# Attention followed by a cosine layer: a fixed order for the layer's second pass, product sums in PSUM, and a plain first sum for weight pair 0

## The chip, the cores and the metric

The kernel runs on one NeuronCore of a Trainium2 chip. The metric is the device time of one execution in microseconds (us), lower is better. The engines are named as in the profile: PE (TensorE, matrix products; PEld is its weight loading), DVE (VectorE), ACT (ScalarE), POOL (GpSimd) and SP (SyncE, which issues most DMAs). PE, DVE and ACT reach PSUM, the banks that matmuls write; POOL works on SBUF alone.

## The reference

Causal attention over 4 batches, 12 heads, 448 positions and 64 columns a head, then a layer with a cosine, all in fp32:

```python
scores = q @ k.T / 8; scores[above the diagonal] = -1e9
x = softmax(scores) @ v            # laid out as 1792 tokens x 768
h = x @ w_in                       # 768 x 2048
g = h * cos(h)
out = g @ w_out                    # 2048 x 768
```

The two weights arrive as 8-byte floats; the kernel reads them as pairs of 32-bit words.

## The kernel before, in words

**Numbers in two parts.** Each fp32 operand of the layer is held as a high part (a cast, made by ACT) and a low part (the rest, by POOL or DVE), both of the type fp32r. A product is three matmuls: high x high, high x low, low x high. `split` (line 594) makes the parts of an activation.

**Attention** (lines 214 to 561) runs 24 pairs of heads, one iteration of its loop each, and three iterations (i = 24, 25, 26) that empty its pipeline. It writes x in two tiles, `xa` for tokens 0 to 1023 and `xb` for 1024 to 1791. After each iteration the loop at lines 1078 to 1101 converts one half of a piece of the first four weight blocks (two of w_in, two of w_out: "weight pair 0"), stores the raw w_out pieces (line 1086) and loads the next piece. In iterations 24 and 25 PE also does the first sums of tokens 0 to 511 (`fill`). Lines 549 to 560 compute four sums q4 of the blocks of w_in's pair 0 on DVE, split them and store them.

**Pass one** (`moe`, `slot`, lines 817 to 878) covers tokens 0 to 1023 in two groups of 512. There are eight weight pairs (two blocks of 128 of the 2048 columns), so sixteen slots k. A slot does the first sum of its group for both blocks (`m1_sum`, 18 matmuls of 512 columns each), the cosine (`cosine_stages`, lines 573 to 585: ACT index, DVE remainder, ACT Sin and Square, DVE final step) and, behind them, the second sum of the slot before (`m2a_chunk`, four chunks of 12 matmuls of 384 columns, with one `add` on DVE each; chunks alternate between two pairs of PSUM banks). Beside that it prepares the weights of the next pair: loads (`fetch`), three mask stages on ACT (line 156, 158, 160), a pack on DVE (lines 167, 171, 175), the two parts (`halve`), the sums of blocks (`first_side`, `side_out`) and the sums of x blocks for pass two (`x_side`). All of it is stored to DRAM. `first_spill` (line 770) stores the four blocks of pair 0 in slots 1 and 2, through SP.

**Pass two** covers tokens 1024 to 1791 as two halves of 384. Each first sum and each second sum is a 2 x 2 product of blocks, done with seven block products instead of eight (Strassen's scheme in Winograd's form), at the price of sums of blocks on both sides. The orders are `SIDE` (first sum) and `MO` (second sum). A round g does these parts:

- `m1b(g)`: seven products of nine matmuls (line 952). The first is copied by ACT to p1 (line 966); `plus` adds the others, on DVE, into SBUF tiles u2, u3, p1, c12, c21, c22; two of the four cosines begin there, reading these tiles.
- `factors`: the other cosines, four sums s1 to s4 of the results on POOL, seven splits (ACT, POOL) into `g_ops`.
- `block_sums(g)`: four sums of the raw w_out blocks on POOL (line 937), from a tile `raw` that is loaded for each pair, with casts on ACT and low halves on DVE or POOL (line 939).
- `m2b(g)`: 21 products of three matmuls (line 1010) in pairs of PSUM banks, each pair added into `accs` by DVE (line 652 through `add`).

Pair 7 is last and is done plainly (`m2_last`), after `combine` has added the 21 accumulators up (line 1025, POOL and DVE).

**What sets the order.** Attention and pass one are inside `with tc.manual_schedule()` (line 1073), so each engine runs them in the order in which the program names them. Pass two runs outside of it (line 1105). There the framework orders the instructions by its own planning, and products of the next round stand between blocks of this one where that planning put them. SP's DMAs have one queue in program order.

Of the kernel before, what the change touches and what calls it, by code (L numbers as in the profile page):

```python
# [20 lines left out]
def kernel(  # L21
# [51 lines left out]
    t_d = spill.tile([9, P, 2, EH], F32, name="t_d")  # L73
# [106 lines left out]
    def spill_halves(kind, f, w, eng=nc.gpsimd):  # L180
        if kind:
            eng.dma_start(out=w_out_d[f], in_=f32(w[:]))
        elif f % 2 == 0:
            eng.dma_start(
                out=w_in_d[f // 2, :, 0:4].rearrange("p b n -> p (b n)"),
                in_=f32(w.rearrange("p u n -> p (u n)")),
            )
        else:
            eng.dma_start(out=side(f // 2, 3), in_=f32(w[:, :, EH:]))

# [23 lines left out]
    def attention(filler):  # L214
        with (
# [261 lines left out]
            for i in range(N + 3):  # L477
# [71 lines left out]
                if i == N:  # L549
                    q4 = at.tile([P, 4, EH], F32, tag="pb", bufs=2, name="q4")  # L550
                    for n, (f, b) in enumerate(((1, 0), (1, 1), (0, 0), (0, 1))):
                        w = ring[0, f][:, :, b * EH : (b + 1) * EH]
                        nc.vector.tensor_tensor(q4[:, n], f32(w[:, 0]), f32(w[:, 1]), op=ALU.add)
                    nc.vector.tensor_tensor(q4[:, 1], q4[:, 0], q4[:, 1], op=ALU.add)
                    nc.vector.tensor_tensor(q4[:, 0], q4[:, 2], q4[:, 0], op=ALU.subtract)
                if i == N + 1:
                    nc.vector.tensor_tensor(q4[:, 2], q4[:, 1], q4[:, 2], op=ALU.subtract)
                    nc.vector.tensor_tensor(q4[:, 3], q4[:, 3], q4[:, 2], op=ALU.subtract)
                    for n, b in ((1, 4), (0, 6), (2, 5), (3, 2)):
                        store_parts(split(q4[:, n], *part_tiles()), side(0, b))  # L560
# [12 lines left out]
    def cosine_stages(hv, n, d=None):  # L573
        ni = gpool.tile([P, 512], I32, tag="ni", bufs=2, name="ni")[:, 0:n]
        r = gpool.tile([P, 512], F32, tag="r", bufs=3, name="r")[:, 0:n]
# [7 lines left out]
        d = r if d is None else d  # L583
        nc.vector.scalar_tensor_tensor(d, r, 1.0, hv, op0=ALU.subtract, op1=ALU.mult)
        yield d
# [51 lines left out]
    def moe(ring, early):  # L637
        with tc.tile_pool(name="mo", bufs=1) as mo:
# [99 lines left out]
            def x_side(i):  # L738
                for t, dst, parts in x_sums:
                    hi, lo = parts or part_tiles()  # L740
                    nc.scalar.copy(hi, t)
                    nc.vector.tensor_tensor(lo, t, f32(hi[:] if parts is None else hi), op=ALU.subtract)
                    if parts is None:
# [392 lines left out]
```

## Time and profile before

| | us |
|---|---|
| three runs of the kernel before | 675.88, 679.0, 681.26 (median 679.0) |
| the profiled execution | 682.1 |
| its span, first to last instruction | 680.3 |
| attention, to the first matmul of pass one | 0 to 172.4 |
| pass one, to the end of its last first sum | 172.4 to 448.7 |
| rest of pass one and pass two | 448.7 to 680.3 |

Rows below have times from the span's start. In a group of instructions, "x54 | 49.4, 946" means 54 instructions, 49.4 us of busy time and a mean of 946 ns; after the second bar stands the idle time of that engine just before them and what ended it. In a timeline, a time in brackets is the idle time before, with its releaser. "out<-in" names the tiles. PE's matmul rows overlap, so their spacing is read from starts. The granted clock (PEclk) is a share of 2.4 GHz.

### The profile page before, as it was taken

The numbers are of one execution on the slowest core, as the hardware profiler recorded it, in microseconds if no ns is written. First come the engines' busy times: TensorE is split into PE (matmuls) and PEld (weight loads), VectorE is DVE, ScalarE is ACT, GpSimd is POOL, SyncE is SP. The second block draws the span as 40 slices with busy tenths as digits, with TensorE's granted clock in tenths as the row PEclk, the third lists the DMA queues.
The fourth block names the chain that finished last, engine by engine and source line by source line (L and its number), as shares of the span: only waits on it lengthen the run. The fifth ranks groups of instructions, "written<-read, shape, count | busy, mean of one in ns | idle before, by whom it ended". The sixth has DMA issues, their size and how long they took to land.

```text
span 680.3 us, 11579 instructions
## 1 busy us (share of the span) xinstructions
PE 640.6 (94%) x3700; PEld 555.2 (82%) x3700; DVE 507.8 (75%) x1102; ACT 429.8 (63%) x958; POOL 441.3 (65%) x425
## 2 busy tenths in 40 slices
PE   8999999999987979999999999999689979999994
PEld 6676776766766969998989899999689879989993
DVE  5888888888537756777777777733886896888796
ACT  5999898989646577777777777530643444545240
POOL 3665666656236767687968796810698987765554
PEclk9999999999987989999999999999979989999997
DMA  5555555455136965878777778599947475564303
GB/s 129 118 116 123 138 123 127 116 127 136 59 96 252 330 242 176 292 241 297 251 265 253 289 252 286 224 370 401 354 116 227 144 254 146 182 208 117 117 1 139
DMA packets 123788, 133.29 MB, mean 196 GB/s; under 512 B 73008, under 2 KB 107936, under 8 KB 123728
## 3 DMA queue, kind: packets, MB, share of 16 engines
q1 hardware_dynamic: 116912, 107.31, 50.8%
q0 software_dynamic: 4928, 24.78, 10.1%
q10 hardware_dynamic: 1888, 0.46, 0.3%
q8 instruction: 30, 0.49, 0.3%
q14 instruction: 30, 0.25, 0.1%
HBM read 82.58 MB, written 49.94 MB: 195 GB/s over the span
## 4 chain that ended last, share of the span: by engine, by line
PE 56%; DVE 14%; POOL 10%; issue 9%; DMA 6%; ACT 4%; POOLq 0%; DVEq 0%; ACTq 0%
PE banks L664 13%; PE banks L436 6%; PE banks L952 5%; PE banks L341 5%; PE banks L569 4%; PE banks L571 4%; PE banks L570 4%; PE banks L1010 4%; PE banks L412 3%; DMA w_in_d<-sh 3%; POOL tr L937 3%; PE banks L350 3%; PE banks L314 3%; DMA raw<-raw_d 3%; DVE acc L652 2%
## 5 line engine op out<-in xcount | busy, mean ns | idle before, releaser
L652 DVE TENSOR_TENSOR acc<-acc,banks 128x768 f32<-128x768 f32 x122 | 111.4, 929 | 46.0 <-PE banks L664 39.9
L664 PE MATMUL banks<-w,gh 128*128 128x384 f32 x512 | 116.4, 350 | 12.5 <-DVE acc L650 4.7
L664 PEld LDWEIGHTS banks<-w,gh 128*128 128x128 f32 x512 | 95.6, 198 | 16.0 <-DVE acc L652 5.8
L390 POOL TENSOR_TENSOR pb<-pb,stat 128x768 f32<-128x768 f32 (+2 forms) x72 | 73.9, 1040 | 42.9 <-ACT flat L324 20.1
L596 POOL TENSOR_TENSOR gl<-r,gh 128x512 fp32r<-128x512 f32 (+1 forms) x48 | 58.9, 1230 | 48.4 <-ACT gh L595 31.1
L372 ACT ACTIVATE pb<-pb,stat 128x384 f32<-128x384 f32 (+1 forms) x144 | 72.4, 511 | 16.1 <-DVE stat L358 16.1
L569 PE MATMUL banks<-xa,w 128*128 128x512 f32 x192 | 75.0, 391 | 0.0
L571 PE MATMUL banks<-xa,w 128*128 128x512 f32 x192 | 75.0, 391 | 0.0
L570 PE MATMUL banks<-xa,w 128*128 128x512 f32 x192 | 75.0, 390 | 0.0
L664 PE MATMUL banks<-w,gl 128*128 128x384 f32 x256 | 67.7, 346 | 0.0
L358 DVE CUSTOM_DVE_ANT_0 pb<-banks,mask 128x384 f32<-128x384 f32 (+1 forms) x144 | 52.9, 418 | 16.6 <-PE banks L341 16.6
L686 POOL TENSOR_TENSOR w<-ct,w 128x768 fp32r<-128x768 f32 x28 | 51.8, 1850 | 10.8 <-DVE r L578 10.2
L1010 PE MATMUL banks<-big,gh 128*128 128x384 f32 x168 | 45.2, 354 | 6.0 <-DVE cs L959 2.7
L1010 PE MATMUL banks<-big 128*128 128x384 f32 x189 | 42.9, 359 | 7.6 <-ACT big L938 5.8
L952 PE MATMUL banks<-xb,bb 128*128 128x384 f32 x261 | 49.6, 335 | 0.3 <-DVE acc L652 0.3
L580 ACT ACTIVATE r<-r 128x512 f32<-128x512 f32 (+1 forms) x64 | 36.9, 576 | 20.4 <-DVE r L578 20.2
L664 PEld LDWEIGHTS banks<-w,gl 128*128 128x128 f32 x256 | 48.6, 197 | 0.2 <-POOL gl L596 0.2
L436 PE MATMUL banks<-pm,vn 128*64 128x448 f32 (+3 forms) x384 | 46.8, 386 | 0.3
L952 PEld LDWEIGHTS banks<-xb,bb 128*128 128x128 f32 x261 | 45.6, 188 | 0.7 <-DVE acc L652 0.6
L436 PEld LDWEIGHTS banks<-pm,vn 128*64 128x64 f32 x384 | 25.4, 136 | 23.1 <-issue 13.0
L1010 PEld LDWEIGHTS banks<-big 128*128 128x128 f32 x189 | 35.9, 204 | 9.9 <-ACT big L938 6.4
L571 PEld LDWEIGHTS banks<-xa,w 128*128 128x128 f32 x192 | 36.0, 188 | 7.6
(154 smaller groups left out, 1565.0 us busy)
## 6 DMA issues: line engine op xcount, KB each, us to landing
bb<-w_in_d SPq DMA_DIRECT2D x50, 384.0 KB, 4.8
land<-in_moe_w_in_dram SPq DMA_DIRECT2D x14, 768.0 KB, 5.2
land<-in_moe_w_out_dram SPq DMA_DIRECT2D x14, 768.0 KB, 5.9
w_out_d<-w POOLq DMA_DIRECT2D x14, 768.0 KB, 5.8
big<-w_out_d SPq DMA_DIRECT2D x25, 384.0 KB, 4.0
w_in_d<-sh SPq DMA_DIRECT2D x32, 192.0 KB, 4.3
w_in_d<-sl SPq DMA_DIRECT2D x32, 192.0 KB, 3.6
w_in_d<-w POOLq DMA_DIRECT2D x7, 768.0 KB, 4.6
```

The source lines that it names most:

```text
L358: nc.vector.tensor_tensor_reduce(out=dst, in0=src, in1=m, scale=-1.0, scalar=3.0e38, op0=ALU.add, op1=ALU.min, accum_out=st[:, 0, n : n + 1],)
L372: nc.scalar.activation(dst, dst, AF.Exp, scale=-1.0, bias=st[:, 0, n : n + 1], accum_out=st[:, 1, n : n + 1],)
L390: nc.gpsimd.tensor_tensor(dst, dst, r.to_broadcast(list(dst.shape)), op=ALU.mult)
L436: nc.tensor.matmul(o[heads(j), kc * P : S], lhsT=vn[:, kc, heads(j)], rhs=pm[:, kc, j, kc * P : S], start=(kc == 0), stop=(kc == NB),)
L569: yield nc.tensor.matmul(hv, lhsT=wh[:, f], rhs=x[:, 0, cc, t], start=(cc == 0), stop=False)
L570: yield nc.tensor.matmul(hv, lhsT=wh[:, f], rhs=x[:, 1, cc, t], start=False, stop=False)
L571: yield nc.tensor.matmul(hv, lhsT=wl[:, f], rhs=x[:, 0, cc, t], start=False, stop=(cc == NCC - 1))
L596: nc.gpsimd.tensor_tensor(lo, r, f32(hi), op=ALU.subtract)
L652: nc.vector.tensor_tensor(d, d, o, op=ALU.subtract)
L664: nc.tensor.matmul(o[:, e, 0:EH], lhsT=a[:, cs], rhs=w[:, e * EH : (e + 1) * EH], start=(x == 0), stop=(x == 5),)
L952: nc.tensor.matmul(o, lhsT=w[:, u, k * P : (k + 1) * P], rhs=x[k][:, v], start=k + n == 0, stop=k == K - 1 and n == 2,)
L1010: nc.tensor.matmul(o[:, b % 2, 0:EH], lhsT=g_ops[i][u][:, c * P : (c + 1) * P], rhs=wouts[g, i][:, v], start=(x == 0), stop=(x == 2),)
```

## The change

In the attention, the q4 sums and their stores go. Each weight block of pair 0 is stored through SP as soon as its last piece is converted there (`spill_halves` in the loop after the iteration), and `first_spill` goes. The third mask stage of the first weight moves from slot 1 to iteration 26. `x_side` stores four kinds of sums in place of three (`t_d` has 12 entries; block b12 of x is kept and loaded over later).

Pass two moves inside the manual order. Its first sum for pair 0 is plain (`plain`, four sums of 18 matmuls on the weight blocks themselves), placed between the last four chunks of pass one. `late_in` issues the loads of pair 0's second sum and of pair 1 after the first sum of slot 15. Each round then has seven steps; a step is one product of the next pair (`product(nx, n)`, nine matmuls), then three products of the second sum (`blocks(g, n)`, nine matmuls), with cosines, sums and loads written out between them. The last sum of each of the four results is added in PSUM (`plus(o, o, ...)`) and the cosine reads it there. The first block of `MO` is now 3. `combine` becomes `merge` calls, five of 21 of them in the last round; the last pair's products are `m2_part`, its outputs `m2_out`.

```diff
-    t_d = spill.tile([9, P, 2, EH], F32, name="t_d")
+    t_d = spill.tile([12, P, 2, EH], F32, name="t_d")
...
-                if i == N:
-                    q4 = at.tile([P, 4, EH], F32, tag="pb", bufs=2, name="q4")
...
-                    for n, b in ((1, 4), (0, 6), (2, 5), (3, 2)):
-                        store_parts(split(q4[:, n], *part_tiles()), side(0, b))
...
-    def cosine_stages(hv, n, d=None):
+    def cosine_stages(hv, n, r=None):
...
-            SIDE = [0, 5, 6, 4, 1, 2, 3]
-            MO = [0, 3, 4, 5, 6, 1, 2]
+            SIDE = [0, 5, 6, 4, 1, 2, 3]
+            MO = [3, 0, 4, 5, 6, 1, 2]
...
+                win_ring.append(tx.pop())
+                for i in (0, 1, 4, 3):
+                    load_in(0, i)
+                for i in range(2 * K):
+                    load_x(tx[i], i)
+                load_in(1, SIDE[0])
+
+            def late_in():
...
+                first_raw()
+                load_out(0)
+                for i in range(3):
+                    load_block(0, i)
+                for i in range(1, 6):
+                    load_in(1, SIDE[i])
+                for i in range(2 * K, 3 * K):
+                    load_x(tx[i], i)
...
-                    some(opening[0])
                     mb = opening[1]
                 run(pack(ia, mo))
-                first_spill()
...
                 run(m1_sum(ring, g, 1, t0, n, hv[1]))
+                if k == 2 * NG - 1:
+                    late_in()
...
+            def plain(f, j, b):
+                o = banks8[:, b, 0:TH]
+                for k in range(2):
+                    w = wins[0, ((0, 1), (4, 3))[f][k]]
+                    for h, x in enumerate(old_x(k, j)):
+                        for n, (u, v) in enumerate(((0, 0), (0, 1), (1, 0))):
+                            nc.tensor.matmul(
...
+            o = plain(0, 1, 2)
+            chunk(0)
+            begin("21", o)
+            go("21")
+            chunk(1)
+            go("21")
+            o = plain(1, 1, 3)
+            for i in range(K):
+                load_x(b12[i], 3 * K + i)
+            chunk(2)
+            begin("22", o)
+            go("22")
+            chunk(3)
+            go("22")
...
-            load_raw(0)
-            load_out(0)
-            load_rest(0)
-            block_sums(0)
-            ready = m1b(0)
-            for g in range(NG):
...
+            for g in range(NG - 1):
+                last = g == NG - 2
+                nx = g + 1
+                load_out(nx)
...
+                sub(nx, 4)
+                a21 = end("21")
+                go("12")
+                w_hi(nx, 4)
+                go("12")
+                fetch_in(0)
+                nc.scalar.copy(p1, product(nx, 0))
+                s1 = less(sm0, a21, c_of["22"], ALU.add)
+                s2 = less(sm1, s1, c_of["11"])
+                hi(g_ops[4], s1)
+                hi(g_ops[5], s2)
+                blocks(g, 0)
+                a12 = end("12")
+                lo(g_ops[4], s1)
+                s3 = less(sm2, c_of["11"], a21)
+                lo(g_ops[5], s2)
...
+                w_lo(nx, 4, nc.vector)
...
+                plus(u2, product(nx, 1), p1)
+                blocks(g, 1)
+                sub(nx, 5)
...
+                plus(u3, product(nx, 2), u2)
+                blocks(g, 2)
+                s4 = less(sm0, a12, s2)
+                sub(nx, 3)
...
+                w_hi(nx, 3)
...
+                o = product(nx, 3)
+                plus(u2, o, u2)
+                plus(o, o, u3)
+                begin("22", o)
+                blocks(g, 3)
+                w_lo(nx, 3, nc.vector)
+                go("22")
+                go("22")
+                sub(nx, 6)
+                w_lo(nx, 5)
+                w_hi(nx, 6)
+                if last:
+                    merge(5, 0, nc.gpsimd)
+                fetch_in(4)
+                if g + 2 < NG - 1:
+                    load_raw(g + 2)
+                o = product(nx, 4)
+                plus(o, o, p1)
+                begin("11", o)
+                blocks(g, 4)
+                r = end("22")
+                go("11")
+                go("11")
+                hi(g_ops[3], r)
+                w_lo(nx, 6)
+                lo(g_ops[3], r)
...
+                o = product(nx, 6)
+                plus(o, o, u3)
+                begin("12", o, c21)
+                blocks(g, 6)
...
+                if half == 1 and j == PARTS - 1:
+                    spill_halves(*key, ring[key], nc.sync)
...
+            elif i == B * NP + 2:
+                some(opening[0])
         run(filler)
-        mixture = moe(ring, early)
-        next(mixture)
-    run(mixture)
+        moe(ring, early)
```

Of the helpers, `begin(name, o)` issues a cosine's index on ACT, the first `go` its remainder on DVE, the second `go` Sin and Square on ACT, and `end` its final step on DVE. `hi` is a cast on ACT and `lo` a low half, on POOL unless an engine is named; `less` is a sum on POOL; `sub`, `w_hi` and `w_lo` make one sum of raw w_out blocks, its cast and its low half. In step 5 (left out) the same is done for "21" as in step 4 for "11", and "11" is ended, cast and given its low half.

## Rows read from the trace of the kernel before

**Rows 1.** The page, busy time of each engine over the span.
```profile
PE 640.6 (94%) x3700; PEld 555.2 (82%) x3700; DVE 507.8 (75%) x1102; ACT 429.8 (63%) x958; POOL 441.3 (65%) x425
```

**Rows 2.** Windows: each engine's busy time (count), then PEclk, DMA share, GB/s.
```profile
200.00:210.00 10.00, 5.34 (x18) 4.80 (x17) 8.29 (x10) 5.96 (x10) 4.86 (x5) 0.67 0.58 181
440.00:460.00 20.00, 20.00 (x105) 18.56 (x105) 7.43 (x9) 5.34 (x9) 5.00 (x5) 1.00 0.99 370
448.73:676.51 227.78, 207.59 (x1114) 199.04 (x1112) 173.53 (x241) 90.10 (x190) 149.74 (x137) 0.95 0.59 197
```

**Rows 3.** Chain that ended last, whole span: start, us, what.
```profile
227.20 13.04 DMA w_in_d<-sh
...
448.89 4.18 PE banks L664 x24
```

**Rows 4.** Timeline of PE, second sums in the opening of pass one.
```profile
194.84 0.87 PE L664 MATMUL banks<-w,gh 128*128 128x384 f32 x4
...
199.28 1.65 PE L664 MATMUL banks<-w,gh 128*128 128x384 f32 x4 [3.21 <-ACT gh L595]
...
209.91 1.65 PE L664 MATMUL banks<-w,gh 128*128 128x384 f32 x4 [4.66 <-DVE acc L650]
...
216.55 0.39 PE L569 MATMUL banks<-xa,w 128*128 128x512 f32 x1
...
241.30 0.87 PE L664 MATMUL banks<-w,gh 128*128 128x384 f32 x4
...
249.88 1.65 PE L664 MATMUL banks<-w,gh 128*128 128x384 f32 x4 [4.24 <-DVE acc L652]
...
256.98 0.39 PE L569 MATMUL banks<-xa,w 128*128 128x512 f32 x1
```

**Rows 5.** Timeline of DVE in the same stretch.
```profile
178.46 1.96 DVE L553 TENSOR_TENSOR q<-w 128x384 f32<-128x384 f32 x4
...
208.90 0.95 DVE L650 TENSOR_SCALAR acc<-banks 128x768 f32<-128x768 f32 x1
```

**Rows 6.** Timeline of ACT in the same stretch.
```profile
182.31 0.41 ACT L147 CAST w<-ct 128x256 fp32r<-128x256 f32 x1 [3.05 <-DVE ct L146]
...
199.13 0.81 ACT L160 ACTIVATE banks<-flat 128x768 f32<-128x768 f32 x1
```

**Rows 7.** DMA issues: count, KB each, median us from issue to landing.
```profile
raw<-raw_d SPq DMA_DIRECT2D x7, 768.0 KB, 6.1
...
w_out_d<-w SPq DMA_DIRECT2D x2, 768.0 KB, 9.0
```

**Rows 8.** Groups by form, 482 to 650 us (rounds of pass two).
```profile
L652 DVE TENSOR_TENSOR acc<-acc,banks 128x768 f32<-128x768 f32 x54 | 49.4, 946 | 5.3 <-PE banks L1010 5.2
...
L937 POOL TENSOR_TENSOR tr<-raw 128x384 f32<-128x384 f32 x14 | 15.8, 1128 | 6.3 <-DMA raw<-raw_d 5.1 <-DVE big L939 1.2
...
L581 ACT ACTIVATE r<-r 128x384 f32<-128x384 f32 x28 | 14.5, 518 | 0.3
...
L578 DVE SCALAR_TENSOR_TENSOR r<-ni,cs 128x384 f32<-128x384 int32 x13 | 12.2, 940 | 1.2 <-ACT ni L576 0.6 <-POOL cs L986 0.4
...
L959 DVE TENSOR_TENSOR u<-banks,u 128x384 f32<-128x384 f32 x14 | 7.7, 552 | 2.2 <-PE banks L952 1.9
```

**Rows 9.** Timeline of all engines: POOL and DVE side by side, then each alone.
```profile
551.64 2.65 POOL L937 TENSOR_TENSOR tr<-raw,tr 128x384 f32<-128x384 f32 x2
...
553.35 1.36 DVE L578 SCALAR_TENSOR_TENSOR r<-ni,cs 128x384 f32<-128x384 int32 x1
...
623.92 0.55 DVE L578 SCALAR_TENSOR_TENSOR r<-ni,acc 128x384 f32<-128x384 int32 x1
...
628.01 1.99 POOL L596 TENSOR_TENSOR gl<-r,gh 128x384 fp32r<-128x384 f32 x2 [6.71 <-ACT gh L595]
```

**Rows 10.** Groups by form, 650 to 682 us.
```profile
L1025 DVE TENSOR_TENSOR acc<-acc 128x384 f32<-128x384 f32 x9 | 10.4, 1188 | 0.2 <-POOL acc L1025 0.2
```

**Rows 11.** Timeline of DVE, its last instruction.
```profile
676.54 0.55 DVE L1042 TENSOR_TENSOR acc<-acc,banks 128x384 f32<-128x384 f32 x1 [2.38 <-PE banks L1036]
```

More of the change, by code (lines that the diff above doesn't have):

```diff
@@ L637, in moe @@
     def moe(ring, early):
+        pend = None
         with tc.tile_pool(name="mo", bufs=1) as mo:
@@ new lines, in chunk, with begin, go, end @@
+            def chunk(c):
+                m2a_chunk(*pend, c)
+            c_of = {}
+            def begin(name, o, r=None):
+                c_of[name] = cosine_stages(o, TH, r)
+                some(c_of[name])
+            def go(name):
+                some(c_of[name])
+            def end(name):
+                (c_of[name],) = c_of[name]
+                return c_of[name]
+            o = plain(0, 1, 2)
[3 more added lines that the diff above has]
+            chunk(1)
@@ L1000, in pair_bank, with blocks @@
-            def pair_bank():
-                b = bank("q", 4, 6, 0, 2)
-                return banks8[:, b : b + 2]
-            def m2b(g):
-                for b in range(21):
-                    i, c = MO[b // 3], b % 3
+            def pair_bank(*places):
+                b = bank("q", *(places or (6, 4)))
+                return banks8[:, b : b + 2]
+            pair = []
+            def blocks(g, n):
+                i = MO[n]
+                for c in range(K):
+                    b = 3 * n + c
@@ new lines, in m2_part @@
+            def m2_part(j, c, o, f, gs):
+                es = [slice(e * EH, (e + 1) * EH) for e in range(2)]
+                gh, gl = gs
+                for x, (a, u) in enumerate(((gh, 0), (gh, 1), (gl, 0))):
+                    for e in range(2):
+                        nc.tensor.matmul(
+                            o[:, e, 0:EH], lhsT=a[:, c * P : (c + 1) * P],
+                            rhs=wouts[NG - 1, f, u][:, es[e]],
+                            start=f == j and x == 0, stop=f == 1 - j and x == 2,
+                        )
@@ new lines, in m2_out @@
+            def m2_out(j, c, o, rows):
+                i = (TA + j * TH) // P + c
+                for e in range(2):
+                    d = part(rows[e], c)
+                    nc.vector.tensor_tensor(d, d, o[:, e, 0:EH], op=ALU.subtract)
+                    nc.sync.dma_start(
+                        out=out[i * P : (i + 1) * P, e * EH : (e + 1) * EH], in_=d
+                    )
+            o = plain(0, 0, 4)
+            begin("11", o)
+            sub(0, 4)
+            r = end("22")
@@ new lines, in moe @@
+            hi(g_ops[3], r)
+            lo(g_ops[3], r)
+            go("11")
+            w_hi(0, 4)
+            go("11")
+            w_lo(0, 4, nc.vector)
+            sub(0, 5)
+            w_hi(0, 5)
+            o = plain(1, 0, 0)
+            load_in(1, SIDE[6])
+            load_raw(1)
+            sub(0, 3)
+            r = end("11")
+            hi(g_ops[0], r)
+            lo(g_ops[0], r)
+            w_hi(0, 3)
+            w_lo(0, 5)
+            sub(0, 6)
+            w_hi(0, 6)
@@ new lines, in moe @@
+            r = end("21")
+            ps = []
+            for c, b in enumerate((6, 4, 2)):
+                o = banks8[:, b : b + 2]
+                m2_part(1, c, o, 1, g_ops[3])
+                ps.append(o)
+            go("12")
+            hi(g_ops[6], r)
+            lo(g_ops[6], r)
+            go("12")
+            r = end("12")
+            merge(6, 5, nc.gpsimd, (2,))
+            hi(g_ops[1], r)
+            lo(g_ops[1], r)
+            merge(3, 6, nc.gpsimd)
+            merge(1, 0, nc.gpsimd)
```

314 lines of the change are left out of this document (151 added, 163 removed).

## The prediction

> **What bounds the kernel now.** I read the page's engine totals first, then the windows, then TensorE's timeline, then the groups. PE is busy for 94% of the span [rows 1], so a change can only win what PE stands idle, what it runs at the low clock, and what the end adds. Pass two holds most of it. From 448.73 us, where the last first sum of pass one ends, to PE's last matmul the stretch is 227.8 us long [rows 2]. It holds 96 matmuls of pass one's second sums and 1,017 of pass two (504 in first sums, 441 in block products, 72 for the last pair). Matmuls of 384 columns stand 0.174 us apart, since 24 of them take 4.18 us [rows 3], so 1,113 need 193.7 us: 34 us are lost there. The opening of pass one loses time as well: the first 48 matmuls of its second sum take 21.7 us (194.84 to 216.55) and the third 48 take 15.7 (241.30 to 256.98) [rows 4], where 48 x 0.174 is 8.4. That is 13.4 + 7.3 = 20.7 us. Some of it is stall (3.2, 4.7 and 4.2 us in [rows 4]), the rest is matmuls at a lower granted clock behind the stalls (0.67 on the mean from 200 to 210 us, between its levels of 1.2 and 2.4 GHz, [rows 2]).
>
> **Edit 1, the side sums of weight pair 0 leave the attention's end.** Eight VectorE operations q4 go (the first four take 1.96 us, [rows 5]), and four splits with eight stores. They hold the conversion that ScalarE waits 3.05 us for, and behind it, in queue order, the first cosine [rows 6]. The third mask stage of the first weight moves too, from behind the second cosine's cast (199.13, [rows 6]) to the attention's last iteration. Followed through by the same durations, ScalarE reaches that stage at about 187.8, VectorE starts to pack at 191.7, and its sums, two more packs and two cosines later, bring the first add to 200.7 instead of 208.90 [rows 5]. PE reaches the third chunk at 194.84 + 24 x 0.174 = 199.0 and waits for that add until 201.6: 2.6 us of the 13.4 stay, and I allow 0.8 for the clock, so 10 us are won. Bounds: 8 if the late chain shifts by its first cause only, 13.4 if nothing waits.
>
> **Edit 2, the first spills move into the attention.** Four transfers leave the first slots, two of them 768 KB from w, landing in 9.0 us [rows 7]. They crowd the queue where ScalarE's cast into a store tile waits 13.04 us for that tile's store [rows 3], which ends in the 4.24 us stall. Without them most of the second loss goes: 7 of 7.3, bounds 0 and 7.3. In the attention they stand on SP ahead of the next loads of q, k and v and of the next weight piece, and SP waits there for GpSimd's low half. Those loads run an iteration ahead of their use, which hides them as long as the queue is emptier there than in the slots. If that cover is gone, each spill costs at most about a third of the 9.0 us that it lands in: bounds 0 and 12 for the four, I take 1. Edits 1 and 2 together: 16 us earlier, between 0 and 20.
>
> **Edit 3, the passage to pass two.** The plain first sum of pair 0 needs eight half products where seven stood: 72 matmuls for 63, 9 x 0.174 = +1.6 us. It needs no sums of inputs, so 4 x 18 matmuls can be placed between the last four chunks of pass one. Loads are early: the four plain weight blocks go first, and about 24 transfers of 384 KB plus eight stores of outputs follow, some 13 MB, which 370 GB/s [rows 2] carries in 35 us, the time until the second product of pair 1. PE could start the first round at 448.73 + (96 + 72) x 0.174 = 477.9. But GpSimd gets its first sums, low halves and casts one behind the other. Counted through at 1.0 us each, w_lo(0, 6) ends near 483.5, and the third block product of round 0 starts 3 us late. The raw weights of pair 1, whose tile is free only when the last chunk has been read, are due at that same moment, 6.1 us after their issue [rows 7]. So +3 (bounds 0 and 8): rounds start at 480.9 on the old clock.
>
> **Edit 4, the seven rounds.** One round is 126 matmuls, 21.9 us on PE. The other engines, by [rows 8]: VectorE ten adds of 0.946, one of half size, eight cosine steps, seven sums and two low halves of 0.55, 19.4; GpSimd seventeen operations at 1.0, 17; ScalarE twenty-four at 0.52, 12.5. So PE is the longest, if nothing loops back. Cosines now read the sum in PSUM. With two SBUF operands a VectorE step beside a busy GpSimd takes 1.36 us and GpSimd's own 1.33; alone, a step takes 0.55 and two GpSimd operations 1.99, so 1.02 each and 0.97 from start to start [rows 9]; with a PSUM operand 0.552 on the average of all [rows 8]. Ten such pairs a round shrink to two (the low halves of blocks 3 and 4), so I take 1.0 for GpSimd (bounds 0.97 and 1.33). For the new in-place sum in PSUM there is no row: 0.55 by the nearest, 1.36 as the other end, on an engine with 2 us to spare. The Trainium skill (Perfetto Trace Analysis, section Optimizing Scalar/DVE Operations) gives VectorE about 60 ns of overhead on SBUF and 125 on PSUM; by that rule eight cosine steps would add 0.5 us a round, 3.6 us in all if it were on the path, and the sum would be 647. The rows show no such difference.
>
> The loop that could be longer than 21.9 runs from GpSimd's third block sum of one round to that of the next: thirteen ScalarE operations (casts, indices, Sin, Square) and the VectorE steps between them, 8.3 us at 0.42 to 0.58 each, then a low half, t4, s1, s2 and eight more on GpSimd, 12 x 0.97 = 11.6, and 0.5 us of waiting for the cast of s1: 20.4 us. That is 1.5 under PE's 21.9, so PE sets the pace, but with banks freed only 0.5 to 1.4 us before their next product. I take 22.5 a round (bounds 21.9 and 25.5): 7 x 22.5 = 157.5, so the last round's matmuls end at 638.4. Loads are 12 transfers of 384 KB a round, under 220 GB/s. The raw tile's reload has 7.2 us from its release (2.1 us into this loop) to its next use (9.3) against 6.1 median [rows 7]: just covered; a late one costs its lateness, about 1 us.
>
> **Edit 5, the end.** Of 21 block additions five move into the last round. From PE's last block product: VectorE's rest of adds and two cosine steps to 3.4, six additions at 1.19 [rows 10] to 10.6, six final subtractions at 0.5 [rows 11] to 13.6, three additions to 15.6, six more subtractions to 18.6. GpSimd's seven additions (ending at 11.6) and PE's 72 matmuls (12.5) lie beside it. From the end of the last subtraction to the span's end it is 3.2 us now (677.1 to 680.3, [rows 11]). So 21.8 us (bounds 20 and 25).
>
> **The sum.** 638.4 + 21.8 = 660.2, less 16 from edits 1 and 2 gives a span of 644.2. The profiled execution ran 682.1 with 680.3 of span, 1.8 around it, so 646.0. It lies 3.1 above the median of the three runs, 679.0, so I forecast 643 us.
>
> **Rivals.**
> A, the forecast: PE sets the rounds and the opening's stalls go. Its own range goes from 630 (20 won before pass two, no late start, 21.9 a round, an end of 20) to 655 (12 won, 2 us more at the start, 23.3 a round).
> B, the fixed order is set by GpSimd's loop. At 1.30 apart twelve or thirteen operations add 4.3 us to 20.4, and with a raw tile 0.8 late it is 25.5 a round: 643 + 7 x 3.0 = 664. For it: GpSimd waits 5.1 us for raw tiles now and its mean is 1.13 there [rows 8]. Against: what slows it are VectorE steps with two SBUF operands, and they go.
> C, the opening gains nothing: the spills delay the attention by as much as they free, or the store tiles wait on (three more x sums are stored). Then 16 us stay: 659, and with 12 us on the attention 671. For it: the DMA queue is on the chain at 227.20 [rows 3]. Against: the stall follows two transfers that leave.
> D, slower than before: the change does not do what it says, since in a fixed order the two rings of waits become one. VectorE's adds wait for PE's block, the cosine behind an add in VectorE's queue waits with it, its cast and low half follow late, and PE waits for the bank that the cosine frees. If each round catches two crossings of 3.1 us (a product and a block) on top of B's 24.7, a round is 30.9 and the time 643 + 7 x 8.4 = 702. It is slower from 22.5 + 36 / 7 = 27.6 us a round. For it: the trace shows one late conversion holding four later ScalarE operations [rows 6]. Against: the queue positions counted above leave each bank free in time.
> The Trainium skill (PSUM — Partial Sum Buffer, section Engine vs sequencer instructions) says that ScalarE's, VectorE's and GpSimd's queues are strictly first in, first out; D is that rule at its worst, and the trace agrees with the rule by those 3.05 us.
>
> **How the numbers follow.** A 0.72, B 0.12, C 0.12, D 0.04. The range 630 to 668 takes in A and B, C's 659, and leaves out D, the worst of C and the worst of B. About 1% can be told from no change: faster than 672 holds A, B and nearly all of C, 0.93; within 1% the worst of C and a round near 27, 0.03; slower D, 0.04.
>
> **What would show it.** Edit 1: the first add of pass one near 200 and under 3 us of PE idle there. Edit 2: no PE stall in the third slot, an attention that ends within 1 us of before. Edit 3: PE without gaps until the first round, then about 3 us. Edit 4: starts of product 0 (the copy to p1) 22 to 23 us apart, VectorE's cosine steps at 0.55, GpSimd near 1.0, a granted clock of 1.0 (2.4 GHz) through the rounds. Edit 5: about 22 us behind the last block product. It is wrong if rounds are over 25.5 us apart, if the attention ends over 3 us late, or if GpSimd's mean stays above 1.15.

## The result and the profile after

The changed kernel takes 645.0 us (median of four runs, 644.46 to 646.04), the kernel before beside it 678.6. The ratio is 0.951, 95% interval 0.947 to 0.955. Forecast were 643.0 us. The profiled execution took 644.5 us with a span of 642.7. Its totals answer to [rows 1], and under them stand the waits of TensorE over the whole span (line and what it waited for: us in total, times, longest).

```profile
PE 623.8 (97%) x3709; PEld 545.0 (85%) x3709; DVE 485.8 (76%) x1087; ACT 427.0 (66%) x953; POOL 428.8 (67%) x421
```

```profile
PE banks L1016 <- DVE r L574: 3.1, 1, 3.1
PE banks L655 <- DVE acc L641: 2.6, 1, 2.6
PE banks L1054 <- DVE acc L1064: 2.0, 1, 2.0
PE banks L316 <- DMA land<-in_q_dram: 1.2, 2, 0.7
...
PE banks L1054 <- ACT ni L567: 1.0, 1, 1.0
...
PE banks L655 <- DVE acc L643: 0.7, 1, 0.7
```

L655 is the second sum of pass one, L1016 a product of a round, L1054 the last pair. PE waits 3.1 us once, in the passage to pass two, and never inside the rounds (L1036, the block products, isn't in the list).

The opening, TensorE's timeline, answers to [rows 4]. The first line is the first chunk, the second the third chunk, the third the same place of the third 48 matmuls.

```profile
196.38 0.87 PE L655 MATMUL banks<-w,gh 128*128 128x384 f32 x4
...
203.35 0.97 PE L655 MATMUL banks<-w,gh 128*128 128x384 f32 x4 [2.62 <-DVE acc L641]
...
237.52 0.98 PE L655 MATMUL banks<-w,gh 128*128 128x384 f32 x4 [0.69 <-DVE acc L643]
```

Before, these stalls were 3.2 and 4.7 us, and 4.2 us [rows 4]. The last first sum of pass one ends at 433.5 us where it ended at 448.7: 15.2 us are won there between these two executions. The price is a first chunk at 196.38, not 194.84: the attention is 1.5 us longer, and the DMA waits of L316 in the list above (1.2 us; the kernel before has none) are part of that.

The passage and the rounds, TensorE's timeline: the last plain sums of pair 0, product 0 and product 1 of round 0, then the third block product (MO[2]) of round 0 and the same of round 6.

```profile
456.44 6.41 PE L911 MATMUL banks<-xb,bb 128*128 128x384 f32 x36
465.99 3.13 PE L1016 MATMUL banks<-xb,bb 128*128 128x384 f32 x9 [3.15 <-DVE r L574]
...
470.53 1.72 PE L1016 MATMUL banks<-tx,big 128*128 128x384 f32 x9
...
475.21 1.03 PE L1036 MATMUL banks<-big 128*128 128x384 f32 x5
...
606.25 1.72 PE L1036 MATMUL banks<-big 128*128 128x384 f32 x9
```

Nine matmuls take 3.13 us behind the stall and 1.72 at full clock: 1.4 us more are lost to the clock (granted 0.53 from 466 to 469 us, near the lower of its two levels, 1.2 GHz). From the third block product of round 0 to that of round 6 it is 131.04 us, 21.84 a round, which is PE's own time (126 matmuls 0.173 us apart). The window over most of the rounds shows it in one line (engines' busy time with counts, then PEclk, DMA share, GB/s), and the groups under it answer to [rows 8].

```profile
484.00:600.00 116.00, 116.00 (x671) 116.00 (x670) 97.61 (x153) 59.71 (x130) 89.07 (x89) 1.00 0.64 225
```

```profile
L574 DVE SCALAR_TENSOR_TENSOR r<-r,banks 128x384 f32<-128x384 f32 x18 | 9.8, 545 | 0.0
L1008 DVE TENSOR_TENSOR banks<-banks,u 128x384 f32<-128x384 f32 x17 | 9.5, 558 | 0.0
L569 DVE SCALAR_TENSOR_TENSOR r<-ni,banks 128x384 f32<-128x384 int32 x17 | 9.3, 548 | 0.9 <-ACT ni L567 0.2
...
L967 POOL TENSOR_TENSOR tr<-raw 128x384 f32<-128x384 f32 x10 | 11.1, 1114 | 0.0
```

PE is busy for all of the 116 us at a granted clock of 1.0. The cosine steps that took 940 ns from SBUF [rows 8] take 548 from PSUM, the new sum in place 558. The end, VectorE's timeline, answers to [rows 10, 11]:

```profile
623.94 7.66 DVE L1047 TENSOR_TENSOR acc<-acc 128x384 f32<-128x384 f32 x6
631.52 2.86 DVE L1064 TENSOR_TENSOR acc<-acc,banks 128x384 f32<-128x384 f32 x6
634.31 1.48 DVE L1047 TENSOR_TENSOR acc<-acc 128x384 f32<-128x384 f32 x3
635.72 1.93 DVE L1064 TENSOR_TENSOR acc<-acc,banks 128x384 f32<-128x384 f32 x4
638.37 1.02 DVE L1064 TENSOR_TENSOR acc<-acc,banks 128x384 f32<-128x384 f32 x2 [0.72 <-PE banks L1054]
```

Six block additions (L1047) take 1.28 us each while GpSimd adds beside them, three take 0.49 each when it is done. PE's last block product ends near 620.3, so the end takes 22.4 us.

### The profile page after: what moved, and what is told of

Same layout as the page of the kernel before. It is cut to its first block, busy times and chain, and to the rows that moved or that the text cites. A ratio compares the mean times of both kernels' runs of the same rounds, so it can differ in the third digit from the quotient of the medians.

```text
span 642.7 us, 11517 instructions
## 1 busy us (share of the span) xinstructions
PE 623.8 (97%) x3709; PEld 545.0 (85%) x3709; DVE 485.8 (76%) x1087; ACT 427.0 (66%) x953; POOL 428.8 (67%) x421
## 4 chain that ended last, share of the span: by engine, by line
PE 69%; DVE 9%; issue 7%; DMA 5%; POOL 4%; ACT 3%; SPq 1%; DVEq 0%; ACTq 0%; POOLq 0%
PE banks L655 12%; PE banks L1016 12%; PE banks L1036 12%; PE banks L438 6%; PE banks L559 5%; PE banks L561 5%; PE banks L560 5%; PE banks L343 4%; PE banks L414 3%; DMA w_in_d<-sh 2%; PE banks L352 2%; DVE pb L360 2%; PE banks L316 2%; POOL w L677 1%; DVE ct L175 1%
## 5 line engine op out<-in xcount | busy, mean ns | idle before, releaser
L643 DVE TENSOR_TENSOR acc<-acc,banks 128x768 f32<-128x768 f32 (+1 forms) x122 | 112.0, 931 | 48.6 <-PE banks L655 39.6
L655 PE MATMUL banks<-w,gh 128*128 128x384 f32 x512 | 110.6, 337 | 3.6 <-DVE acc L641 2.6
L655 PEld LDWEIGHTS banks<-w,gh 128*128 128x128 f32 x512 | 90.4, 188 | 7.0 <-DVE acc L641 2.9
L655 PE MATMUL banks<-w,gl 128*128 128x384 f32 x256 | 65.2, 335 | 0.0
L571 ACT ACTIVATE r<-r 128x512 f32<-128x512 f32 (+1 forms) x56 | 32.8, 586 | 38.9 <-DVE r L569 38.9
L586 POOL TENSOR_TENSOR gl<-r,gh 128x512 fp32r<-128x512 f32 x32 | 41.6, 1300 | 20.9 <-ACT gh L585 20.6
L567 ACT ACTIVATE ni<-banks 128x512 int32<-128x512 f32 (+1 forms) x64 | 34.3, 536 | 28.0 <-PE banks L561 13.8
L1016 PE MATMUL banks<-xb,bb 128*128 128x384 f32 x234 | 46.2, 342 | 3.1 <-DVE r L574 3.1
L655 PEld LDWEIGHTS banks<-w,gl 128*128 128x128 f32 x256 | 46.4, 188 | 0.0
L974 POOL TENSOR_TENSOR gl<-r,gh 128x384 fp32r<-128x384 f32 x16 | 16.2, 1015 | 44.1 <-ACT gh L971 41.3
L569 DVE SCALAR_TENSOR_TENSOR r<-ni,banks 128x512 f32<-128x512 int32 (+1 forms) x56 | 35.0, 625 | 13.9 <-ACT ni L567 13.1
L1016 PEld LDWEIGHTS banks<-xb,bb 128*128 128x128 f32 x234 | 42.1, 193 | 3.5 <-DVE r L574 3.5
L574 DVE SCALAR_TENSOR_TENSOR r<-r,banks 128x512 f32<-128x512 f32 (+1 forms) x56 | 35.0, 625 | 12.8 <-ACT r L572 12.8
```

The source lines that it names most:

```text
L643: nc.vector.tensor_tensor(d, d, o, op=ALU.subtract)
L655: nc.tensor.matmul(o[:, e, 0:EH], lhsT=a[:, cs], rhs=w[:, e * EH : (e + 1) * EH], start=(x == 0), stop=(x == 5),)
L1016: nc.tensor.matmul(o, lhsT=w[:, u, k * P : (k + 1) * P], rhs=x[k][:, v], start=k + m == 0, stop=k == K - 1 and m == 2,)
```

## The experiments

Each run is a version of the changed kernel. Ratios are to the kernel before, so 0.951 is "no difference from the changed kernel"; two ratios whose intervals overlap are told apart by the trace, if at all. For the opening I use the start of the first plain sum, 441.9 us in the changed kernel: over it and the seven runs below that change nothing ahead of that point and keep pass two in its fixed order it lies between 440.1 and 445.4 (mean 442.6), so less than some 3 us there means nothing.

**Opening: the q4 sums.** All of the removed work of edit 1 is back but the mask stage.

```diff
+if i == N:
+    q4 = at.tile([P, 4, EH], F32, tag="pb", bufs=2, name="q4")
...
+if i == N + 1:
...
+    for n, d in ((1, t_d[12]), (0, side(0, 6)), (2, side(0, 5)), (3, side(0, 2))):
+        store_parts(split(q4[:, n], *part_tiles()), d)
```

> The changed kernel with the removed work of the attention's end put back as work that nothing reads: the eight VectorE sums q4, their four splits and eight stores; the mask stage stays where the change put it. Theory (the q4 sums hold the conversion and the first cosine behind them, which makes most of the late first add): the first add of pass one comes 6 to 9 us later than the 203.3 less 0.95 us of the changed kernel, and the time is 6 to 10 us longer, best value +8, 653. Rival (the mask stage was what counted, and the sums lie beside other work): within 2 us of 645.

Measured: 654.1 us, ratio 0.965 (0.961 to 0.969), and the first plain sum at 451.3. The two stalls of [rows 4] are back, in TensorE's timeline:

```profile
201.09 1.65 PE L667 MATMUL banks<-w,gh 128*128 128x384 f32 x4 [4.77 <-ACT gh L597]
...
210.22 1.65 PE L667 MATMUL banks<-w,gh 128*128 128x384 f32 x4 [3.41 <-DVE acc L653]
```

The sums, with their splits and stores, cost 9 us; which of the three it is, no run separates. **The mask stage**, put back alone:

```diff
 else:
+    some(opening[0])
     mb = opening[1]
...
-elif i == B * NP + 2:
-    some(opening[0])
```

> The changed kernel with the third mask stage of the first weight back in slot 1, behind the second cosine's cast; the q4 sums stay out. Theory (both parts lie on one chain, the mask stage with its 0.8 us and the wait in ScalarE's queue behind the late cast): the first add of pass one comes 2 to 4 us later and the time is 2 to 5 us longer, best value +3, 648. Rival (the stage waits for nothing once the q4 sums are gone): within 1 us of 645.

Measured: 645.9 us, ratio 0.953 (0.949 to 0.957). The stall is 2.62 us, the same, and the first add comes 5.97 us behind the first chunk (202.49 and 196.52), as in the changed kernel (202.35 and 196.38). The theory falls: with the q4 work gone, moving the stage wins nothing; what edit 1 wins is the q4 work.

**Opening: the first spills** back in slots 1 and 2.

```diff
-if half == 1 and j == PARTS - 1:
-    spill_halves(*key, ring[key], nc.sync)
...
 run(pack(ia, mo))
+first_spill()
...
 run(pb)
+first_spill()
```

> The changed kernel with the four first spills back in slots 1 and 2. Theory (the prediction's edit 2): the stall of TensorE in the third slot, 0.7 us in the changed kernel, comes back to about 4 us with matmuls at the lower clock behind it, +7 us, and the attention ends 1.5 us earlier: +5.5 us in all, 650.5 (647 to 653). Rival (the eight q4 stores that left did it, and the spills only move): the attention's 1.5 us come back and nothing else, 643.5.

Measured: 648.0 us, ratio 0.957 (0.953 to 0.961); the profiled span is 649.0. The stall of the third 48 matmuls is back, in TensorE's timeline (the changed kernel has 0.69 us there):

```profile
240.03 1.65 PE L655 MATMUL banks<-w,gh 128*128 128x384 f32 x4 [3.99 <-DVE acc L643]
```

The stall follows ScalarE's cast into a store tile, which waits for that tile's store. ScalarE's timelines of the kernel before, of the changed kernel and of this run show that wait:

```profile
240.32 0.51 ACT L595 CAST sh<-ct 128x384 fp32r<-128x384 f32 x1 [8.63 <-DMA w_in_d<-sh]
```

```profile
226.72 0.51 ACT L585 CAST sh<-ct 128x384 fp32r<-128x384 f32 x1 [3.86 <-DMA w_in_d<-sh]
```

```profile
230.46 0.51 ACT L585 CAST sh<-ct 128x384 fp32r<-128x384 f32 x1 [8.40 <-DMA w_in_d<-sh]
```

The rival, that the q4 stores made this stall, falls with the run that put them back: there the cast waits 3.79 us and PE 0.47.

The first chunk comes at 194.33; with early spills it comes between 194.8 and 197.1, at 195.9 on the mean of nine executions. The first plain sum starts at 447.3, 4.7 us later than the mean above. That is near the 5.5 expected; by the medians it is 3 us, and by the intervals it could be little. What is shown is the mechanism: the stall goes with the spills. The attention pays 1 to 2 us for them: the mean of 195.9 against 194.33 here and 194.84 before, one execution each.

**Rounds: the cosine sums in SBUF again.**

```diff
-plus(o, o, u3)
-begin("22", o)
+plus(c22, o, u3)
+begin("22", c22)
```

(and so for 11, 21 and 12, in p1, c12 and u3).

> The changed kernel, but each of the four cosine sums of a round is formed in SBUF again, as before the change, and not over the product in PSUM; order, counts of instructions and banks stay. Theory (contention price, the prediction's term of 0.55 us for a cosine step from PSUM): the eight cosine steps of a round on VectorE then read two fp32 operands from SBUF and take about 0.9 us in place of 0.55 where GpSimd runs beside them, and GpSimd's operations get longer too, so that the loop over GpSimd, ScalarE and VectorE, put at 20.4 us, grows to 23 to 25 us and paces the round in TensorE's place: 1 to 3 us a round, 7 to 20 us in all, the best single value +12 us, time 657. Rival (TensorE paces a round with so much to spare that the price is hidden): the steps get longer but TensorE has no idle time inside the rounds, time 645 to 647.

Measured: 658.0 us, ratio 0.970 (0.967 to 0.973): +13 us, the expected value nearly to the microsecond. Its window over the same stretch, and the groups of VectorE:

```profile
484.00:600.00 116.00, 108.41 (x608) 104.30 (x606) 107.53 (x137) 54.60 (x116) 90.43 (x83) 1.00 0.59 209
```

```profile
L569 DVE SCALAR_TENSOR_TENSOR r<-ni,acc 128x384 f32<-128x384 int32 x5 | 6.8, 1368 | 0.0
L569 DVE SCALAR_TENSOR_TENSOR cs<-ni,u 128x384 f32<-128x384 int32 x5 | 6.8, 1361 | 0.0
...
L569 DVE SCALAR_TENSOR_TENSOR r<-ni,cs 128x384 f32<-128x384 int32 x5 | 2.7, 546 | 0.0
```

A step with two SBUF operands takes 0.55 us where GpSimd happens to be idle and 1.36 where it isn't. The copies to p1 stand 23.9 us apart (540.98 to 588.86 for two rounds). VectorE is busy 107.5 of 116 us. The theory named the loop over GpSimd, ScalarE and VectorE; with VectorE at 93% it may as well be VectorE's queue alone that paces the rounds, and no run separates the two.

**Rounds: how long is the loop of the other engines?** One and three more subtractions on GpSimd in each round:

```diff
 s4 = less(sm0, a12, s2)
+for _ in range(3):
+    less(accs[10][:, 1], a12, s2)
```

> The changed kernel with one more GpSimd subtraction of 128x384 in each round, right ahead of the raw difference behind block product 2; its result goes to a plane that nothing reads. Theory (the loop over GpSimd, ScalarE and VectorE takes 20.4 us, under the 21.84 us of TensorE in a round): 1.0 us more fits into the 1.4 us of slack, time within 1.5 us of 645. Rival (GpSimd's queue is already on the path at this place, since the block products wait for the low halves that it writes): 1 us a round, +7 us, 652.

> The same as the run with one more subtraction, with three in each round. Theory (loop of 20.4 us): 20.4 + 3.0 = 23.4 us paces the round, 1.6 us more than TensorE, +11 us over seven rounds, time 656 (650 to 660). Rival (GpSimd's idle stretches, 4 to 5 us a round in the trace, take the extra work, so that the loop was put too long in the prediction): within 2 us of 645.

Measured: 648.7 us, ratio 0.956 (0.952 to 0.960) with one, 661.4 us, 0.975 (0.970 to 0.979) with three. Both are above what the theory allowed (within 1.5 us of 645; 650 to 660). ScalarE's timelines, the copy to p1 in rounds 1 and 5, first with one, then with three:

```profile
496.27 0.46 ACT L1111 COPY p<-banks 128x384 f32<-128x384 f32 x1
...
585.61 0.46 ACT L1111 COPY p<-banks 128x384 f32<-128x384 f32 x1
```

```profile
495.68 0.46 ACT L1111 COPY p<-banks 128x384 f32<-128x384 f32 x1
...
593.88 0.46 ACT L1111 COPY p<-banks 128x384 f32<-128x384 f32 x1
```

Four rounds take 89.34 and 98.20 us: 22.33 and 24.55 a round. Two subtractions are 2.22 us, so one is 1.11 on this path, and without any the loop takes an estimated 22.33 - 1.11 = 21.2 us, if the path stays the same. The rival of the second run, the idle stretches, falls: a round grows by the whole of each further subtraction, so GpSimd's idle time is waiting inside the loop. The rival of the first run, that GpSimd is already on the path, asks for 1 us a round; it is 0.5 (22.33 less 21.84). The loop exists, as predicted, but is near 21.2 us and not 20.4, and PE's 21.84 covers it by 0.6 us, not by 1.5.

**Rounds: the order.** Pass two by the planner again, alone and with the cosine sums in SBUF:

```diff
+yield
 o = plain(0, 1, 2)
...
-    moe(ring, early)
+    mixture = moe(ring, early)
+    next(mixture)
+run(mixture)
```

> The changed kernel, but pass two (from the plain first sums on) is ordered by the planner again and not in the order of the text; the instructions are the same. Theory (the fixed order itself carries most of what the rounds won): the planner's order gives back between a third and all of it, +8 to +25 us, best value +15, time 660, with idle time of TensorE between the first sums and the block products. Rival (what was won lies in the removed instructions and in the PSUM sums, and the planner finds an order as good): time 643 to 648.

> Both reversals together: pass two is ordered by the planner and its four cosine sums of a round are formed in SBUF. What stays of the change in pass two are the plain first sum of pair 0, the removed copies and the moved ends. Theory (the two add up, since the price of two SBUF operands, 12.9 us in the fixed order, is paid by engines and not by an order): 645.0 + 5.4 + 12.9 = 663 (659 to 668). Rival (the planner, free to move work, hides the dearer steps beside TensorE, so that the PSUM sums are worth it only in a fixed order): 650 to 655.

Measured: 650.4 us, ratio 0.958 (0.954 to 0.961) with the planner alone, 657.6 us, 0.969 (0.966 to 0.971) with both. Both theories were too high and both rivals too low. With the planner PE is busy for 127.8 of the 132 us from 484 to 616, where the changed kernel has 132.0; the waits come in small pieces (L1037, the block products) and at the end (L1055, where the changed kernel waits 2.0):

```profile
PE banks L1055 <- DVE acc L1065: 3.6, 2, 2.3
PE banks L1037 <- DVE acc L643: 3.1, 6, 0.9
```

So the order that the change writes by hand, from the plain sums on, is worth about 5 us (none of the planner's four times, 646.8 to 651.5, is as short as one of the changed kernel's, 644.5 to 646.0), and only together with the PSUM sums: with sums in SBUF the planner's order (657.6) and the fixed one (658.0) are equal. Why is not shown; VectorE is busy for 123.1 us of the 132 in the fixed order and for 113.4 in the planner's. The PSUM sums are worth 13 us in the fixed order and 7 in the planner's.

**Passage: the wait of 3.1 us.** It is a queue wait: the step that frees bank 2 (L574) stands on VectorE behind a low half (L974) that waits 2.04 us for a cast. VectorE's timeline of the changed kernel:

```profile
464.68 0.80 DVE L974 TENSOR_TENSOR big<-tr,big 128x384 fp32r<-128x384 f32 x1 [2.04 <-ACT big L971]
465.40 0.54 DVE L574 SCALAR_TENSOR_TENSOR r<-r,banks 128x384 f32<-128x384 f32 x1
```

Moved ahead:

```diff
+end("21")
 o = plain(1, 1, 3)
...
-a21 = end("21")
+a21 = end("21") if g else c_of["21"]
```

> The changed kernel with one instruction moved in the passage to pass two: the last cosine step of result 21 of pair 0, which frees bank 2 for product 0 of the first round, stands ahead of the second plain sum in VectorE's queue, not behind a low half that waits for a cast. Theory (the wait of 3.1 us is a matter of queue order at one place, but GpSimd's queue stands next: its first sum of the round is behind the raw tile's landing at 469.7, so that the low halves for the third block product are ready near 474 and 476): the stall moves to the third block product and shrinks, a gain of 1 to 2 us, 643.5. Rival (nothing else is late): the 3.1 us and the half-speed product behind them (1.4 us) go, 640.5. If bank 2 was not the cause: 645.

Measured: 645.1 us, ratio 0.952 (0.948 to 0.956): nothing. TensorE's timeline shows the stall in pieces further on; the last line is the third block product:

```profile
463.97 1.72 PE L1017 MATMUL banks<-xb,bb 128*128 128x384 f32 x9
466.01 0.44 PE L1037 MATMUL banks<-big,gh 128*128 128x384 f32 x1 [0.32 <-ACT big L972]
466.83 0.45 PE L1037 MATMUL banks<-big,gh 128*128 128x384 f32 x1 [0.38 <-DVE big L975]
...
471.07 0.62 PE L1037 MATMUL banks<-big,gh 128*128 128x384 f32 x2 [0.49 <-DVE acc L641]
...
476.05 2.69 PE L1037 MATMUL banks<-big 128*128 128x384 f32 x9 [2.10 <-DVE acc L641]
```

It starts 12.1 us behind the end of the plain sums (476.05 less 463.97), in the changed kernel 12.5 (475.21 less 462.68, the end of the 36 matmuls from 456.44); PE alone needs 7.8 for what lies between. The bank wait stood in front of a longer one. The row names VectorE's add, but that add stands behind a cosine step, which waits for ScalarE, whose cast waits for GpSimd's first difference of pair 1. GpSimd reaches that difference late, at 470.98, and the last 0.71 us before it are a wait for the raw tile's landing.

**GpSimd's work moved ahead:** in the passage it waits 16.9 us for a cast, while the raw weights of pair 0 have landed. GpSimd's timeline of the changed kernel:

```profile
460.73 1.01 POOL L974 TENSOR_TENSOR gl<-r,gh 128x384 fp32r<-128x384 f32 x1 [16.93 <-ACT gh L971]
```

The run moves the four weight differences of pair 0 into that wait, frees bank 2 early and loads the raw tile of pair 1 earlier:

```diff
+def early_sum(i, eng=nc.gpsimd):
+    sub(0, i)
+    w_hi(0, i)
+    w_lo(0, i, eng)
...
 o = plain(0, 1, 2)
+early_sum(4)
+early_sum(5)
...
+early_sum(3)
+early_sum(6)
+end("21")
...
 chunk(3)
...
+load_raw(1)
...
-sub(0, 4)
...
-w_hi(0, 4)
...
-w_lo(0, 4, nc.vector)
...
```

(with the first use of the raw tile of pair 1 moved behind `blocks(0, 1)`.)

> The changed kernel with the passage to pass two put in another order: the four weight differences of pair 0 with their casts and low halves are issued between the last chunks of pass one, where GpSimd is idle for 16.9 us; the raw tile of pair 1 is loaded right behind the last chunk and first used behind the second block product of round 0; bank 2 is freed early as in the run with that step moved. Theory (GpSimd's queue is what holds the third block product of round 0 in the changed kernel and in that run): the third block product starts 7.8 us behind the last plain sum and not 12.5 us, TensorE has no idle time in the passage, time 645.0 - 4.5 = 640.5 (639 to 642). Rival (the transfers set the passage, since the queue carries 400 GB/s from 430 to 462 us): a wait for a DMA takes the place of the others, gain under 1 us, 644.5.

Measured: 641.8 us, ratio 0.946 (0.943 to 0.949). TensorE's timeline: product 0, the third block product, and a wait behind the moved low half.

```profile
463.94 1.72 PE L1027 MATMUL banks<-xb,bb 128*128 128x384 f32 x9
...
471.74 1.72 PE L1047 MATMUL banks<-big 128*128 128x384 f32 x9
...
476.31 1.32 PE L1047 MATMUL banks<-big 128*128 128x384 f32 x6 [0.76 <-DVE acc L641]
```

The third block product starts 7.8 us behind the plain sums. GpSimd's queue was the cause, with what it waited for: the run also brings the raw tile earlier, and the two are not told apart.

**The end.**

```diff
 if last:
+    merge(1, 0, nc.gpsimd)
     merge(5, 0, nc.gpsimd)
...
 blocks(g, 4)
+if last:
+    merge(6, 5, nc.gpsimd, range(2))
...
-merge(5, 4, nc.vector)
...
 for c in range(K):
+    merge(3, 6, nc.vector, (c,))
+    merge(4, 6, nc.vector, (c,))
     m2_out(1, c, ps[c], (3, 4))
```

> The changed kernel with the 21 block additions of the end in another order and on other engines: twelve or more of them on GpSimd in the last round and beside the last pair's products, six on VectorE, each just ahead of the output that reads it; one low half moves from GpSimd to VectorE. Theory (behind the last block product TensorE's 72 matmuls of 12.5 us are the least that the end can take, and its wait of 2.0 us and the outputs wait for VectorE's six additions of 1.28 us): the end shrinks from 22.4 us to 18 to 20 us, time 645.0 - 3.3 = 641.7. Rival (GpSimd's additions slow VectorE's beside them, 1.28 us in place of about 0.5, as much as they take off it, or the additions in the last round delay the low halves that the block products wait for): 644 to 647.

Measured: 643.7 us, ratio 0.947 (0.944 to 0.951), not to be told from the changed kernel by the times alone. In the trace the end takes 18.5 us (last block product to 624.1, span 642.6) in place of 22.4, and PE's wait of 2.0 us is gone; but this execution began pass two at 445.4, 3.5 us later than the changed kernel's. **Both together**, and the low half that made the 0.76 us wait moved behind `blocks(0, 2)`:

> Both new orders together, the one of the passage and the one of the end, and the low half of round 0 that held VectorE's queue for 2.7 us in the run of the new passage moved behind the third block product. Theory (the two gains lie at different ends of pass two, with TensorE's pace between them, so they add): 645.0 - 3.2 - 2.2 - 0.8 = 638.8 (637 to 640.5), with TensorE without idle time from the passage to the end of the rounds. Rival (what one wins the other loses, since the rounds run closer to the loop of the other engines): 641 to 643.

Measured: **636.0 us** (635.8 to 639.2, six runs), ratio 0.937 (0.935 to 0.940). It beats both kernels, and the theory by 2.8 us, more than its range allowed. The reason is in the traces: the third block product comes at 470.56 (4.65 us earlier) and the end takes 18.5 us (3.9 less), together 8.6, the difference of the spans, 642.7 and 634.1. The theory had put in 4.0 us for the passage and 2.2 for the end, where the traces show 4.65 and 3.9: both were sized too low. From the passage to the end of the rounds PE hardly stops:

```profile
460.00:480.00 20.00, 20.00 (x117) 20.00 (x117) 14.02 (x20) 9.92 (x22) 16.38 (x16) 1.00 0.87 327
484.00:616.00 132.00, 131.81 (x761) 131.49 (x759) 109.25 (x169) 65.80 (x143) 105.40 (x105) 1.00 0.54 184
```

## Why the prediction was right

The forecast was a span of 644.2 and the trace has 642.7. The terms, one by one:

- **Edits 1 and 2**, 16 us forecast: 15.2 measured, between two single executions of which the one before was 3.1 us above its median. By medians it is less: the run with the q4 work back is 9.1 us longer and the one with late spills 3.0, 12.1 together. The stall that stays in the third chunk is 2.62 us, forecast 2.6; the first add comes at 202.35, which is 200.8 without the longer attention, forecast 200.7. One point was wrong: I counted the mask stage as part of the chain, and the run with the stage back shows that it lies beside the chain once the q4 sums are gone. The spills' part was 7 of 7.3 for 1 us of attention; 1.1 of the 7.3 is left (48 matmuls from 232.49 to 241.90 us, less 8.35), and the attention pays 1.5. One row was misread: 13.04 us is how long the store took, and ScalarE's cast waited 8.63 us of it; the cause was right. The rival that the opening gains nothing falls with the two runs that bring its stalls back.
- **Edit 3**, rounds 3 us late: 3.3 measured (465.99 + 15.2 = 481.2 on the old clock, less 477.9, which is 478.0 by its own terms). That the size agrees is luck: the first wait is another one than I named, bank 2 at product 0, on VectorE behind a cast. The run that frees it shows the forecast wait, the third block product behind GpSimd's backlog, in its place, and that product nearly as late. What I left out is the clock behind the stall, 1.4 us.
- **Edit 4**, 22.5 us a round: this term was sized 0.66 us a round too high. Inside the rounds PE waits for nothing, 21.84 us a round, so PE sets the pace. I had allowed for late banks because the loop was near, and the loop is even nearer than counted (about 21.2, not 20.4), but a loop that is shorter at all costs nothing. Of the price of contention, on which the rival with 25.5 us a round rested, VectorE's part was rightly read (1.36 us a step with sums in SBUF) and GpSimd's was not: its mean is 1.00 us in the changed kernel (89.07 us for 89) and 1.09 even with sums in SBUF (90.43 for 83), not 1.30, and a round then takes 23.9 us. The slower side (rings of waits in a fixed order) doesn't occur; the fixed order is 5 us better than the planner's.
- **Edit 5**, 21.8 us: 22.4 measured. Additions at 1.19 were 1.28 beside GpSimd.

Of the forecast span, 0.8 us too little stood for the opening, 0.3 for the passage and 0.6 for the end; 3.2 too much for the rounds (154.3 us from their start to the last block product, the 1.4 of the clock included, for 157.5). That leaves 1.5 us of span, and the kernel's median lies 2 us above the forecast because the profiled execution isn't 3.1 us above the median this time but 0.6 below it. So the closeness of the number is in part luck: the rounds' error covers those of the other terms, and part of the offset's. That PE sets the rounds and that the opening's stalls go is not luck; the waits of PE and the runs show both. Two of the signs set down ahead were missed by a little: the rounds are 21.84 us apart and not 22 to 23, and the attention ends 1.5 us later and not within 1.

Two rules can now be weighed. The Trainium skill (SBUF — State Buffer, section SBUF: two separate sides) says that VectorE and GpSimd hold a shared pair of ports exclusively, VectorE only in some modes or with two SBUF inputs. The runs agree: 1.36 us against 0.55 with two SBUF inputs, 0.55 with one from PSUM, whatever GpSimd does. The other rule of the Trainium skill (Perfetto Trace Analysis, section Optimizing Scalar/DVE Operations), about 125 ns of overhead for VectorE on PSUM against 60 on SBUF, isn't seen: 546 ns for an undisturbed step from SBUF, 545 to 548 from PSUM.

## What to carry to other kernels

Where VectorE works beside a busy GpSimd, let its elementwise steps read one operand from PSUM: eight such steps a round were worth 13 us here, and a fixed order was worth something only once they were cheap. A wait that a trace names may stand in front of a longer one, as bank 2 did: count the queue behind it to its next due time before moving anything, and move what an idle engine could have done earlier. Where the bounding engine has no slack in the rounds, what is left lies at the two ends of the stage; nine microseconds were there.

## What was not expected of the hardware

The price of a short wait of PE differs from one execution to the next, with the same instructions. The changed kernel and the run with the new end are the same up to the last round. In the changed kernel the wait of 2.62 us in the opening is followed by matmuls at full clock (four in 0.97 us, granted clock 1.00 from 195 to 210 us). In the run with the new end the wait is 2.63 us, and four matmuls take 1.65 us. Its TensorE timeline and its window:

```profile
204.05 1.65 PE L655 MATMUL banks<-w,gh 128*128 128x384 f32 x4 [2.63 <-DVE acc L641]
```

```profile
195.00:210.00 15.00, 12.37 (x53) 11.67 (x52) 9.95 (x13) 10.67 (x16) 10.98 (x10) 0.78 0.51 184
```

The granted clock there is 0.78: a part of the stretch is at the lower of the two levels, 1.2 GHz and not 2.4. In the passage the waits of 3.15 and 2.10 us are followed by slow matmuls (3.13 and 2.69 us for nine, against 1.72), the one of 0.76 us hardly (1.32 us for six, against 1.20). This is one source of the scatter in the opening. Others are the first chunk, which comes between 194.8 and 197.1 us, and the stall of the third 48 matmuls, 0.56 to 1.87 us in executions with the same opening. Whether the three make all of the 5 us was not tried.
